# A window-attention kernel: gradient loads on GpSimd's queue, turns by identity matmul, and another order of the products in a pair

## The chip, the cores and the metric

The kernel runs on one core of a Trainium2 chip. The metric is the device time of one execution in microseconds (us); lower is better. "Faster" or "slower" needs 2%; what is nearer counts as "the same".

In the profile PE is TensorE (PEld its weight loads), DVE is VectorE, ACT is ScalarE, POOL is GpSimd and SP is SyncE. SyncE does no arithmetic here: it only issues DMA transfers, one after the other. `SPq`, `POOLq` and `ACTq` are the three engines' issue queues.

## The reference

Attention in windows of 8x8 pixels of a 256x256 image with C = 384 channels, forward and backward, in bf16:

```python
xw  = windows_8x8(x)                       # (1024, 64, 384)
qkv = xw @ wqkv
p   = softmax(einsum('bqc,bkc->bqk', q, k) * C ** -0.5)
o   = einsum('bqk,bkc->bqc', p, v) @ wo    # windows put back into the image
# outputs: o, and the gradients of x, wqkv and wo for a given grad_out
```

## The kernel before

Before the loop the four weight products are folded, so that a window needs only products with 384x384 matrices. The loop takes 4 double windows (128 tokens each, a "quad") per step, 128 steps and a few partial ones at the ends. It is a software pipeline written out by hand: each engine executes its instructions in the order of the program. A step works on three quads at once: `A` is being projected, `B` is in its softmax and its first pair of products, `C_` gets its second pair.

`x` and `grad_out` come in as tiles `xq` and `dq`; DMA transposes turn them into `xT` and `dT`, and the projected `yz` into `tok`. All these are issued by SyncE. Results leave through `osb` and `dsb`, stored by GpSimd. Every PSUM tile comes out of one ring of 8 banks, one bank a tile, so a matmul that starts a tile waits until the bank's last user has been copied out.

```python
    ob = ctx.enter_context(tc.tile_pool(name="ob", bufs=3))      # osb (tag "o") and dsb (tag "d"): 3 each
    ring = ctx.enter_context(tc.tile_pool(name="ring", bufs=8, space=bass.MemoryType.PSUM))
    # ... cut; G_ON_PE is 0, so the loop over grad_turn below does nothing ...
    def load(st):
        bp, t0 = st["at"]
        st["xq"] = xq = grp.tile([P, QUAD, C], BF16, tag="xq", name="xq", bufs=2 * GQ + 4)
        st["dq"] = dq = qp.tile([P, QUAD, C], BF16, tag="dq", name="dq", bufs=6)
        for t in range(QUAD):
            nc.sync.dma_start(out=xq[:, t, :], in_=dram_tile(x, bp, t0 + t))
            nc.sync.dma_start(out=dq[:, t, :], in_=dram_tile(grad_out, bp, t0 + t))

    def load_turn(st):
        xq, dq = st["xq"], st["dq"]
        st["xT"] = xT = qp.tile([P, QUAD, CK, P], BF16, tag="xT", name="xT", bufs=3)
        st["dT"] = dT = qp.tile([P, QUAD, CK, P], BF16, tag="dT", name="dT")
        for src, dst in ((dq, dT), (xq, xT)):
            k = G_ON_PE if src is dq else 0
            if k < QUAD:
                nc.sync.dma_start_transpose(out=dst[:, k:].rearrange("p t m k -> p (t m) k"),
                                            in_=src[:, k:].rearrange("p t c -> p (t c)"))

    # ... cut: project (TensorE, dT or xT -> yz), to_tokens (SyncE, yz -> tok), scores, soft, uv ...

    def turn(st, kind):
        n = ("PT", "ST")[kind]
        st[n] = dst = qp.tile([P, QUAD, WT], BF16, tag=n, name=n)
        pt = ring.tile([P, QUAD, WT], BF16, tag="r")
        for t in range(QUAD):
            for w, o, h in ((0, LO, HI), (1, HI, LO)):
                if kind == 0:
                    nc.tensor.transpose(pt[o, t, :], st["Pb"][o, t, :], ident[o, o])
                else:
                    nc.tensor.transpose(pt[o, t, :], st["ps"][h, w, t, :], ident[h, h])
        nc.vector.tensor_copy(out=dst[:], in_=pt[:])

    def attend(st, pair):
        bp, t0 = st["at"]
        if pair[0] == 0:
            st["Uq"] = grp.tile([P, QUAD, C], BF16, tag="Uq", name="Uq")
            st["Wq"] = grp.tile([P, QUAD, C], BF16, tag="Wq", name="Wq")
        pds = []
        for t in pair:
            pd = ring.tile([P, C], F32, tag="r", name="pd")
            for w, o in ((0, HI), (1, LO)):
                nc.tensor.matmul(pd[o, :], lhsT=st["ps"][:, w, t, :], rhs=st["tok"][:, :, t, w, :], start=True,
                                 stop=False)
            pds.append(pd)

        def both(t, straight, crossed):
            for h, o, (dst, lhs, rhs, first) in ((LO, LO, straight), (LO, HI, crossed), (HI, LO, crossed),
                                                 (HI, HI, straight)):
                nc.tensor.matmul(dst[o, :], lhsT=st[lhs][h, t, :], rhs=st[rhs][h, t, :], start=first, stop=True)

        for t, pd in zip(pair, pds):
            po = ring.tile([P, C], F32, tag="r", name="po")
            pu = ring.tile([P, C], F32, tag="r", name="pu")
            pw = ring.tile([P, C], F32, tag="r", name="pw")
            both(t, (pu, "ST", "xq", True), (po, "PT", "uq", True))
            osb = ob.tile([P, C], BF16, tag="o")
            ENG[EV["o"][t]](out=osb[:], in_=po[:])
            ENG[EV["U"][t]](out=st["Uq"][:, t, :], in_=pu[:])
            both(t, (pw, "Pb", "dq", True), (pd, "ST", "vq", False))
            dsb = ob.tile([P, C], BF16, tag="d")
            ENG[EV["d"][t]](out=dsb[:], in_=pd[:])
            for dst, src in ((out_0, osb), (out_1, dsb)):
                for h, w in ((LO, 1), (HI, 0)):
                    nc.gpsimd.dma_start(out=dram_tile(dst, bp, t0 + t)[WIN * w:WIN * (w + 1)], in_=src[h, :])
            ENG[EV["W"][t]](out=st["Wq"][:, t, :], in_=pw[:])

    # ... cut: gf_group, whose parts ("fillers") are 12 matmuls and one fp32 addition to GF_acc on VectorE ...

    def step(c, b, a):
        # ... cut ...
        C_, B, A = on(c), on(b), on(a)
        B(scores)
        B(soft, 0)
        B(uv, 0, 0)
        B(uv, 0, 1)
        B(soft, 1)
        B(uv, 1, 0)
        B(uv, 1, 1)
        B(soft, 2)
        B(soft, 3)
        B(uv, 2, 0)
        B(uv, 2, 1)
        for t in range(QUAD):
            A(grad_turn, t)
        B(uv, 3, 0)
        B(uv, 3, 1)
        B(soft, 4)
        for mo in range(CK):
            A(project, 0, mo)
        B(soft, 5)
        filler(1)
        C_(attend, (2, 3))
        B(turn, 0)
        B(turn, 1)
        for mo in range(CK):
            A(project, 1, mo)
        A(to_tokens)
        filler(1)
        B(attend, (0, 1))

    # copies out of PSUM: "A" ScalarE, "D" VectorE
    EV = {"z": "AAA", "y": "AAA", "u": "AAAA", "v": "AAAA", "o": "AAAA", "U": "DDDD", "W": "DDDD", "d": "AAAA"}
```

The products in `attend` use the 128x128 array in three ways. The score and projection matmuls use all of it. `po`, `pu`, `pw` and half of `pd` are 64x64 products, four of which run side by side. The other half of `pd` has 128 rows and 64 columns: the "K=128 products".

Of the kernel before, what the change touches and what calls it, by code (L numbers as in the profile page):

```python
# [11 lines left out]
BF16 = mybir.dt.bfloat16  # L12
F32 = mybir.dt.float32

P = 128
WIN = 8
WT = WIN * WIN
QUAD = 4
# [4 lines left out]
def kernel(  # L23
# [21 lines left out]
    nc = tc.nc  # L45
    _, H, W, C = x.shape
# [13 lines left out]
    ring = ctx.enter_context(tc.tile_pool(name="ring", bufs=8, space=bass.MemoryType.PSUM))  # L60

    ident = const.tile([P, P], BF16)
# [8 lines left out]
    for jm in range(JK):  # L71
        pt = ring.tile([P, C], BF16, tag="r")
# [4 lines left out]
    for mo in range(CK):  # L77
        pt = ring.tile([P, C], BF16, tag="r")
# [8 lines left out]
    for dst, left, lo, right, ro, sc in (  # L87
# [5 lines left out]
        for mr in range(CK):  # L93
            pc = ring.tile([P, C], F32, tag="r")
            for mc in range(CK):
                nc.tensor.matmul(pc[:], lhsT=left[:, lo + mc, mr * P:(mr + 1) * P], rhs=right[:, ro + mc, :],
                                 start=(mc == 0), stop=(mc == CK - 1))
# [8 lines left out]
    def dram_tile(ap, bp, t):  # L106
        return ap[0, 2 * WIN * bp:2 * WIN * (bp + 1), WIN * t:WIN * (t + 1), :]

    LO, HI = slice(0, WT), slice(WT, P)
    OTHER = {0: HI, WT: LO}  # L110
# [4 lines that stand above are left out]
        st["dq"] = dq = qp.tile([P, QUAD, C], BF16, tag="dq", name="dq", bufs=6)  # L115
        for t in range(QUAD):
            nc.sync.dma_start(out=xq[:, t, :], in_=dram_tile(x, bp, t0 + t))  # L117
            nc.sync.dma_start(out=dq[:, t, :], in_=dram_tile(grad_out, bp, t0 + t))  # L118

    def load_turn(st):  # L120
        xq, dq = st["xq"], st["dq"]
# [16 lines left out]
    ENG = {"D": nc.vector.tensor_copy, "A": nc.scalar.copy}  # L138
# [31 lines left out]
    def over_k(ap, n=P):  # L170
        return ap.unsqueeze(2).broadcast_to([n, QUAD, WT])

    def soft(st, step):
        sd = st["sd"]
        if step == 0:
# [47 lines left out]
    def turn(st, kind):  # L223
        n = ("PT", "ST")[kind]
        st[n] = dst = qp.tile([P, QUAD, WT], BF16, tag=n, name=n)
        pt = ring.tile([P, QUAD, WT], BF16, tag="r")
        for t in range(QUAD):
            for w, o, h in ((0, LO, HI), (1, HI, LO)):
                if kind == 0:
                    nc.tensor.transpose(pt[o, t, :], st["Pb"][o, t, :], ident[o, o])  # L230
                else:
                    nc.tensor.transpose(pt[o, t, :], st["ps"][h, w, t, :], ident[h, h])
        nc.vector.tensor_copy(out=dst[:], in_=pt[:])

    def attend(st, pair):
        bp, t0 = st["at"]
        if pair[0] == 0:
            st["Uq"] = grp.tile([P, QUAD, C], BF16, tag="Uq", name="Uq")
            st["Wq"] = grp.tile([P, QUAD, C], BF16, tag="Wq", name="Wq")
        pds = []  # L240
        for t in pair:
            pd = ring.tile([P, C], F32, tag="r", name="pd")
            for w, o in ((0, HI), (1, LO)):
                nc.tensor.matmul(pd[o, :], lhsT=st["ps"][:, w, t, :], rhs=st["tok"][:, :, t, w, :], start=True,  # L244
                                 stop=False)
            pds.append(pd)

        def both(t, straight, crossed):
            for h, o, (dst, lhs, rhs, first) in ((LO, LO, straight), (LO, HI, crossed), (HI, LO, crossed),
                                                 (HI, HI, straight)):  # L250
                nc.tensor.matmul(dst[o, :], lhsT=st[lhs][h, t, :], rhs=st[rhs][h, t, :], start=first, stop=True)  # L251

        for t, pd in zip(pair, pds):
            po = ring.tile([P, C], F32, tag="r", name="po")
            pu = ring.tile([P, C], F32, tag="r", name="pu")
            pw = ring.tile([P, C], F32, tag="r", name="pw")
            both(t, (pu, "ST", "xq", True), (po, "PT", "uq", True))
            osb = ob.tile([P, C], BF16, tag="o")
            ENG[EV["o"][t]](out=osb[:], in_=po[:])  # L259
            ENG[EV["U"][t]](out=st["Uq"][:, t, :], in_=pu[:])  # L260
            both(t, (pw, "Pb", "dq", True), (pd, "ST", "vq", False))
            dsb = ob.tile([P, C], BF16, tag="d")
            ENG[EV["d"][t]](out=dsb[:], in_=pd[:])  # L263
            for dst, src in ((out_0, osb), (out_1, dsb)):
                for h, w in ((LO, 1), (HI, 0)):
                    nc.gpsimd.dma_start(out=dram_tile(dst, bp, t0 + t)[WIN * w:WIN * (w + 1)], in_=src[h, :])  # L266
            ENG[EV["W"][t]](out=st["Wq"][:, t, :], in_=pw[:])  # L267

    fill = []

# [12 lines left out]
    def filler(n):  # L283
        while n and fill:
            try:
                next(fill[0])
                n -= 1
            except StopIteration:
                fill.pop(0)

    def step(c, b, a):


        def on(st):
            return (lambda f, *r: f(st, *r)) if st is not None else (lambda f, *r: None)
# [18 lines that stand above are left out]
            A(project, 0, mo)  # L314
        B(soft, 5)
        filler(1)
        C_(attend, (2, 3))
        B(turn, 0)
        B(turn, 1)
        for mo in range(CK):  # L320
            A(project, 1, mo)
        A(to_tokens)
        filler(1)
        B(attend, (0, 1))

    G_ON_PE = 0
    EV = {"z": "AAA", "y": "AAA", "u": "AAAA", "v": "AAAA", "o": "AAAA", "U": "DDDD", "W": "DDDD", "d": "AAAA"}
    quads = [(bp, t0) for bp in range(NBP) for t0 in range(0, NT, QUAD)]
    sts = [{"at": q, "i": i} for i, q in enumerate(quads)]
    n = len(sts)  # L330
    AHEAD = 3
    with tc.manual_schedule(engines=MANUAL):
        for i in range(min(AHEAD, n)):
            load(sts[i])
            if i < AHEAD - 1:
                load_turn(sts[i])
        held = []
        get = lambda i: sts[i] if 0 <= i < n else None
        for i in range(-1, n + 1):
            if AHEAD <= i + AHEAD < n:  # L340
                load(sts[i + AHEAD])
            if AHEAD - 1 <= i + AHEAD - 1 < n:
                load_turn(sts[i + AHEAD - 1])
            step(get(i - 1), get(i), get(i + 1))
            if i > 0:
                held.append(sts[i - 1])
                sts[i - 1] = None
            if held and (len(held) == GQ or i == n):
                fill.append(gf_group(held))
                held = []  # L350
        filler(1 << 30)
# [3 lines left out]
    for f in range(2):  # L355
        nc.vector.tensor_copy(out=GFb[:, f, :, :], in_=GF_acc[:, f, :, :])
        for mb in range(CK):
            pt = ring.tile([P, C], BF16, tag="r")
# [4 lines left out]
    for ma in range(CK):  # L363
        for i, (lhs, f, rhs, r0) in enumerate(((GFT, 0, w_sb, C), (GFb, 0, w_sb, 0), (GFT, 1, woT_sb, 0))):
            pe = ring.tile([P, C], F32, tag="r")
            for mb in range(CK):
                nc.tensor.matmul(pe[:], lhsT=lhs[:, f, mb, ma * P:(ma + 1) * P], rhs=rhs[:, mb, r0:r0 + C],
                                 start=(mb == 0), stop=(mb == CK - 1))
# [6 lines left out]
    for mc in range(CK):  # L375
        pe = ring.tile([P, C], F32, tag="r")
        for ma in range(CK):
            nc.tensor.matmul(pe[:], lhsT=w_sb[:, ma, 2 * C + mc * P:2 * C + (mc + 1) * P], rhs=GFb[:, 1, ma, :],
                             start=(ma == 0), stop=(ma == CK - 1))
# [32 lines left out]
```

## Time and profile before

| before | |
|---|---|
| time, median of 3 runs | 2145.26 us (2143.43 to 2146.45) |
| TensorE busy | 95% of the span |
| from the start of one step's score matmuls to the next | fastest 15.785, median 16.108, mean 16.389 us |
| sum of SyncE's DMA issues | 2006 us |
| TensorE idle before the first matmul that reads dT | 54.2 us |

The steps are those 123 in which every stage has work; they are read off the timeline. First, four lines of the page of the kernel before. The last is from the list of DMA issues: size of one transfer, and median us from issue to landing.

```profile
span 2144.9 us, 50954 instructions
PE 2029.8 (95%) x18814; PEld 1098.6 (51%) x18814; DVE 1379.5 (64%) x3235; ACT 1448.5 (68%) x3213; POOL 1137.8 (53%) x2054
...
L147 PE MATMUL pj<-dT,BT_sb 128*128 128x512 bf16 x1152 | 276.6, 387 | 60.4 <-DMA dT<-dq 54.2
...
dq<-in_grad_out_dram SPq DMA_DIRECT2D x512, 96.0 KB, 3.3
```

TensorE is nearly always busy, and of its idle time one group alone has 60.4 us, 54.2 of them ended by the transpose that makes dT. The view of waits (who waits, for whom: total us, times, longest) shows that beside another, much larger wait:

```profile
PE pj L147 <- DMA dT<-dq: 54.2, 58, 3.4
...
ACT osb L259 <- DMA out_dram<-osb: 180.6, 84, 2.4
...
ACT dsb L263 <- DMA out_dram<-dsb: 6.4, 6, 2.6
```

By this label ScalarE spends 180.6 us waiting for an `osb` buffer whose store has not landed. The label is an inference of the view (it names whatever event came last), and here it is wrong: followed one by one in the trace, the last store from the same buffer had landed at least 3.5 us before each of these 84 copies, and the copy began a median 0.09 us after the last matmul into its `po` had ended. ScalarE, busy for 68%, was waiting for TensorE. For `dsb` the 6 waits are real waits for a buffer by this test: each copy began within 0.2 us of the landing of the store from its own buffer.

Why is dT late? Here is SyncE's queue over one step, in the timeline (start us, duration us, engine, line, operation, count, and in brackets idle time before it, of which there is none here):

```profile
1006.75 6.27 SPq L156 DMA_TRANSPOSE tok<-yz  x1
1013.06 0.59 SPq L117 DMA_DIRECT2D xq<-in_x_dram  x1
1013.69 0.60 SPq L118 DMA_DIRECT2D dq<-in_grad_out_dram  x1
...
1018.20 2.17 SPq L127 DMA_TRANSPOSE dT<-dq  x1
1020.42 1.99 SPq L127 DMA_TRANSPOSE xT<-xq  x1
1022.51 5.35 SPq L156 DMA_TRANSPOSE tok<-yz  x1
```

Each issue starts 0.04 to 0.10 us after the one before it has ended: the queue has no pause at all. Summed over the run: tok 703, xT 362, xq 335, dq 323, dT 282, with three single transfers 2006 us of 2145. SyncE is a second engine at its limit, beside TensorE, though the page counts it as no engine at all.

Last, the end of a pair and the next step's scores, in the timeline:

```profile
1001.44 0.35 PE L251 MATMUL po<-uq,PT 64*64 64x384 bf16 x2
...
1001.88 0.48 ACT L259 CAST osb<-po 128x384 bf16<-128x384 f32 x1 [2.15 <-DMA out_dram<-osb]
...
1001.96 0.33 PE L251 MATMUL pd<-vq,ST 64*64 64x384 bf16 x2
...
1002.41 0.28 PE L165 MATMUL sd<-xT,yz 128*128 128x64 bf16 x4
```

The last products start at 1001.96, the scores only 0.45 us later. They begin 0.05 us after ScalarE has finished `osb` (1001.88 + 0.48 = 1002.36): by this a wait for a PSUM bank, though it looks like the price of a change of array mode. The copy itself began 0.09 us after `po` was finished (1001.44 + 0.35 = 1001.79); the store that its label names was not that of its buffer, which had landed at 996.07.

### The profile page before, as it was taken

To read this page: it belongs to the slowest core of one execution; us is meant where nothing else is said; L and a number is where in the kernel's file an instruction comes from. 1 tells how busy PE (TensorE), PEld (TensorE's weight loads), DVE (VectorE), ACT (ScalarE), POOL (GpSimd) and SP (SyncE) were. 2 spreads that over 40 slices of the span, in tenths; PEclk is the share of its full clock that TensorE was granted. 3 is DMA by queue.
4 is the path that set the end of the run, shared out by engine and by line. 5 is a ranking of instruction groups with operands and counts; after the bars stand their busy time and mean duration, and the time that the engine had idled before them with its cause. 6 is when DMAs were issued, how large, how long until landed. Compare 5 with 4: busy or idle time off the path is not lost.

```text
span 2144.9 us, 50954 instructions
## 1 busy us (share of the span) xinstructions
PE 2029.8 (95%) x18814; PEld 1098.6 (51%) x18814; DVE 1379.5 (64%) x3235; ACT 1448.5 (68%) x3213; POOL 1137.8 (53%) x2054
## 2 busy tenths in 40 slices
PE   7899999999999999999999999999999999999998
PEld 4455555555555555555545555554555555455544
DVE  4566666666666666666666666666666666666665
ACT  5676676767666766666766767676766667676663
POOL 1555555555555555555554555555555455555544
PEclk9999999999999999999999999999999999999999
DMA  8999999999999999999999999999999999999992
GB/s 171 198 192 197 192 196 196 192 193 199 193 193 196 200 191 195 191 196 193 198 190 190 198 191 202 193 197 188 197 198 196 190 198 194 192 198 194 190 184 76
DMA packets 1046330, 409.04 MB, mean 191 GB/s; under 512 B 880704, under 2 KB 1028928, under 8 KB 1046080
## 3 DMA queue, kind: packets, MB, share of 16 engines
q1 hardware_dynamic: 947376, 304.17, 80.9%
q0 software_dynamic: 98304, 101.32, 18.2%
q8 instruction: 147, 2.41, 0.5%
q14 instruction: 103, 0.84, 0.1%
q10 hardware_dynamic: 400, 0.29, 0.0%
HBM read 101.84 MB, written 101.84 MB: 95 GB/s over the span
## 4 chain that ended last, share of the span: by engine, by line
PE 41%; DMA 26%; SPq 15%; ACT 9%; issue 5%; POOL 1%; DVE 1%; ACTq 0%; POOLq 0%
DMA dT<-dq 20%; PE pj L147 16%; PE pj L219 10%; PE pg L278 9%; SPq L117 7%; SPq L118 7%; DMA out_dram<-osb 5%; ACT yz L150 4%; ACT osb L259 3%; PE sd L165 3%; POOL out_dram L266 1%; SPq L156 1%; DMA out_dram<-dsb 1%; ACT yz L152 1%; PE pd L244 1%
## 5 line engine op out<-in xcount | busy, mean ns | idle before, releaser
L266 POOL DMA_DIRECT2D out_dram<-osb x1024 | 571.9, 563 | 933.6 <-ACT osb L259 906.3
L266 POOL DMA_DIRECT2D out_dram<-dsb x1024 | 571.9, 563 | 51.2 <-issue 20.5
L259 ACT CAST osb<-po 128x384 bf16<-128x384 f32 x512 | 249.8, 488 | 408.4 <-DMA out_dram<-osb 180.6
L280 DVE TENSOR_TENSOR GF_acc<-pg,GF_acc 128x384 f32<-128x384 f32 x258 | 143.9, 558 | 542.7 <-PE pg L278 542.7
L278 PEld LDWEIGHTS <-xq 128*128 128x128 bf16 x3072 | 300.0, 98 | 226.8 <-issue 1.6
L219 PEld LDWEIGHTS <-xT 128*128 128x128 bf16 x3072 | 291.9, 98 | 185.5 <-issue 3.6
L219 PE MATMUL pj<-B_sb,xT 128*128 128x384 bf16 x1536 | 334.6, 327 | 1.8 <-ACT dsb L263 1.8
L219 PE MATMUL pj<-AT_sb,xT 128*128 128x384 bf16 x1536 | 334.0, 327 | 0.0
L147 PE MATMUL pj<-dT,BT_sb 128*128 128x512 bf16 x1152 | 276.6, 387 | 60.4 <-DMA dT<-dq 54.2
L260 DVE CAST Uq<-pu 128x384 bf16<-128x384 f32 x512 | 283.0, 553 | 75.3 <-PE pu L251 75.3
L267 DVE CAST Wq<-pw 128x384 bf16<-128x384 f32 x512 | 280.5, 548 | 0.0
L221 ACT CAST uq<-pj 128x384 bf16<-128x384 f32 x512 | 247.5, 483 | 41.9 <-PE pj L219 37.5
L278 PE MATMUL pg<-Uq,xq 128*128 128x384 bf16 x1536 | 270.5, 326 | 0.1
L278 PE MATMUL pg<-Wq,xq 128*128 128x384 bf16 x1536 | 270.1, 326 | 0.1
L147 PE MATMUL pj<-xT,A_sb 128*128 128x512 bf16 x1152 | 269.2, 379 | 0.6
L263 ACT CAST dsb<-pd 128x384 bf16<-128x384 f32 x512 | 254.7, 497 | 7.6 <-DMA out_dram<-dsb 6.4
L221 ACT CAST vq<-pj 128x384 bf16<-128x384 f32 x512 | 250.2, 489 | 2.8 <-PE pj L219 0.5
L152 ACT CAST yz<-pj 128x512 bf16<-128x512 f32 x384 | 224.2, 585 | 32.0 <-PE pj L147 0.9
L150 ACT CAST yz<-pj 128x512 bf16<-128x512 f32 x384 | 208.4, 638 | 14.4 <-PE pj L147 13.3
L147 PEld LDWEIGHTS <-BT_sb 128*128 128x128 bf16 x1152 | 106.8, 99 | 207.2 <-DMA dT<-dq 92.2
L198 ACT COPY ps<-Pb 64x256 bf16<-64x256 bf16 x256 | 103.2, 403 | 149.6 <-DVE Pb L195 148.1
L251 PE MATMUL pu<-xq,ST 64*64 64x384 bf16 x1024 | 175.5, 336 | 0.0
(64 smaller groups left out, 2217.4 us busy)
## 6 DMA issues: line engine op xcount, KB each, us to landing
xq<-in_x_dram SPq DMA_DIRECT2D x512, 96.0 KB, 3.2
dq<-in_grad_out_dram SPq DMA_DIRECT2D x512, 96.0 KB, 3.3
out_dram<-osb POOLq DMA_DIRECT2D x1024, 48.0 KB, 3.8
out_dram<-dsb POOLq DMA_DIRECT2D x1024, 48.0 KB, 4.4
dT<-dq SPq DMA_TRANSPOSE x128, 6.5
xT<-xq SPq DMA_TRANSPOSE x128, 7.1
tok<-yz SPq DMA_TRANSPOSE x128, 7.9
w_sb<-in_wqkv_dram SPq DMA_DIRECT2D x1, 864.0 KB, 5.5
```

Of the source, the lines that this page charges most:

```text
L147: nc.tensor.matmul(pj[:].rearrange("p t w k -> p (t w k)"), lhsT=wgt[:, m, mo * P:(mo + 1) * P], rhs=src[:, :, m, :], start=(m == 0), stop ...
L150: ENG[EV["z"][mo]](out=yz[:, mo, :, 0:4:3, :], in_=pj[:])
L152: ENG[EV["y"][mo]](out=yz[:, mo, :, 1:3, :], in_=pj[:])
L219: nc.tensor.matmul(pj[:], lhsT=st["xT"][:, t, m, :], rhs=wgt[:, m, :], start=(m == 0), stop=(m == CK - 1))
L221: cp(out=dst[:, t, :], in_=pj[:])
L251: nc.tensor.matmul(dst[o, :], lhsT=st[lhs][h, t, :], rhs=st[rhs][h, t, :], start=first, stop=True)
L259: ENG[EV["o"][t]](out=osb[:], in_=po[:])
L260: ENG[EV["U"][t]](out=st["Uq"][:, t, :], in_=pu[:])
L263: ENG[EV["d"][t]](out=dsb[:], in_=pd[:])
L266: nc.gpsimd.dma_start(out=dram_tile(dst, bp, t0 + t)[WIN * w:WIN * (w + 1)], in_=src[h, :])
L267: ENG[EV["W"][t]](out=st["Wq"][:, t, :], in_=pw[:])
L278: nc.tensor.matmul(pw[:], lhsT=st["xq"][:, t, ma * P:(ma + 1) * P], rhs=st["UW"[f] + "q"][:, t, :], start=(i == 0), stop=(i == n - 1))
```

## The change

The intent has two parts. The gradient loads leave SyncE's full queue for GpSimd's. And in a pair of tiles the products are put in an order that is meant to have fewer changes of array mode: the turns of P and dS, now identity matmuls, come first, then all 64x64 products, then the K=128 products, so that the output `dsb` (the gradient of x) is finished, copied and stored last.

```diff
--- before.py
+++ after.py
@@ -115,7 +115,7 @@
         st["dq"] = dq = qp.tile([P, QUAD, C], BF16, tag="dq", name="dq", bufs=6)
         for t in range(QUAD):
             nc.sync.dma_start(out=xq[:, t, :], in_=dram_tile(x, bp, t0 + t))
-            nc.sync.dma_start(out=dq[:, t, :], in_=dram_tile(grad_out, bp, t0 + t))
+            nc.gpsimd.dma_start(out=dq[:, t, :], in_=dram_tile(grad_out, bp, t0 + t))
 
     def load_turn(st):
         xq, dq = st["xq"], st["dq"]
@@ -223,48 +223,45 @@
     def turn(st, kind):
         n = ("PT", "ST")[kind]
         st[n] = dst = qp.tile([P, QUAD, WT], BF16, tag=n, name=n)
-        pt = ring.tile([P, QUAD, WT], BF16, tag="r")
+        pt = ring.tile([P, QUAD, WT], F32, tag="r", name="pt")
         for t in range(QUAD):
             for w, o, h in ((0, LO, HI), (1, HI, LO)):
-                if kind == 0:
-                    nc.tensor.transpose(pt[o, t, :], st["Pb"][o, t, :], ident[o, o])
-                else:
-                    nc.tensor.transpose(pt[o, t, :], st["ps"][h, w, t, :], ident[h, h])
+                lhs, h = (st["Pb"][o, t, :], o) if kind == 0 else (st["ps"][h, w, t, :], h)
+                nc.tensor.matmul(pt[o, t, :], lhsT=lhs, rhs=ident[h, h], start=True, stop=True)
         nc.vector.tensor_copy(out=dst[:], in_=pt[:])
+
+    def store(dst, src, bp, t):
+        for h, w in ((LO, 1), (HI, 0)):
+            nc.gpsimd.dma_start(out=dram_tile(dst, bp, t)[WIN * w:WIN * (w + 1)], in_=src[h, :])
 
     def attend(st, pair):
         bp, t0 = st["at"]
         if pair[0] == 0:
             st["Uq"] = grp.tile([P, QUAD, C], BF16, tag="Uq", name="Uq")
             st["Wq"] = grp.tile([P, QUAD, C], BF16, tag="Wq", name="Wq")
-        pds = []
+        def both(straight, crossed):
+            for h, o, (dst, lhs, rhs, done) in ((LO, LO, straight), (LO, HI, crossed), (HI, LO, crossed),
+                                                (HI, HI, straight)):
+                nc.tensor.matmul(dst[o, :], lhsT=st[lhs][h, t, :], rhs=st[rhs][h, t, :], start=True, stop=done)
+
+        made = []
         for t in pair:
-            pd = ring.tile([P, C], F32, tag="r", name="pd")
-            for w, o in ((0, HI), (1, LO)):
-                nc.tensor.matmul(pd[o, :], lhsT=st["ps"][:, w, t, :], rhs=st["tok"][:, :, t, w, :], start=True,
-                                 stop=False)
-            pds.append(pd)
-
-        def both(t, straight, crossed):
-            for h, o, (dst, lhs, rhs, first) in ((LO, LO, straight), (LO, HI, crossed), (HI, LO, crossed),
-                                                 (HI, HI, straight)):
-                nc.tensor.matmul(dst[o, :], lhsT=st[lhs][h, t, :], rhs=st[rhs][h, t, :], start=first, stop=True)
-
-        for t, pd in zip(pair, pds):
-            po = ring.tile([P, C], F32, tag="r", name="po")
-            pu = ring.tile([P, C], F32, tag="r", name="pu")
-            pw = ring.tile([P, C], F32, tag="r", name="pw")
-            both(t, (pu, "ST", "xq", True), (po, "PT", "uq", True))
+            po, pu, pw, pd = [ring.tile([P, C], F32, tag="r", name=n) for n in ("po", "pu", "pw", "pd")]
+            both((pu, "ST", "xq", True), (po, "PT", "uq", True))
             osb = ob.tile([P, C], BF16, tag="o")
             ENG[EV["o"][t]](out=osb[:], in_=po[:])
             ENG[EV["U"][t]](out=st["Uq"][:, t, :], in_=pu[:])
-            both(t, (pw, "Pb", "dq", True), (pd, "ST", "vq", False))
+            both((pw, "Pb", "dq", True), (pd, "ST", "vq", False))
+            ENG[EV["W"][t]](out=st["Wq"][:, t, :], in_=pw[:])
+            made.append((t, pd))
+            store(out_0, osb, bp, t0 + t)
+        for t, pd in made:
+            for w, o in ((0, HI), (1, LO)):
+                nc.tensor.matmul(pd[o, :], lhsT=st["ps"][:, w, t, :], rhs=st["tok"][:, :, t, w, :], start=False,
+                                 stop=True)
             dsb = ob.tile([P, C], BF16, tag="d")
             ENG[EV["d"][t]](out=dsb[:], in_=pd[:])
-            for dst, src in ((out_0, osb), (out_1, dsb)):
-                for h, w in ((LO, 1), (HI, 0)):
-                    nc.gpsimd.dma_start(out=dram_tile(dst, bp, t0 + t)[WIN * w:WIN * (w + 1)], in_=src[h, :])
-            ENG[EV["W"][t]](out=st["Wq"][:, t, :], in_=pw[:])
+            store(out_1, dsb, bp, t0 + t)
 
     fill = []
 
@@ -314,9 +311,9 @@
             A(project, 0, mo)
         B(soft, 5)
         filler(1)
-        C_(attend, (2, 3))
         B(turn, 0)
         B(turn, 1)
+        C_(attend, (2, 3))
         for mo in range(CK):
             A(project, 1, mo)
         A(to_tokens)
```

## The prediction

> **What bounds it now.** Part 1 of the page has TensorE busy for 95%, but the 128 near-equal steps tell more. From one step's score matmuls to the next (timeline), the fastest quarter take 15.79 us, the mean is 16.39. Nearly all of the 0.60 us between, 76 us in the run, is idle before one matmul, the first that reads dT (waits view: PE for DMA dT<-dq 54 us, 58 times). The transposes come late because the SyncE queue is full: its issues, added up over the timeline, take 703 (tok) + 362 (xT) + 335 (xq) + 323 (dq) + 282 (dT) = 2006 us, with some 0.04 us between them 16.2 us a step. So SyncE sets the pace and TensorE, at 15.79, is just under it.
>
> **Loads moved.** This takes 4 x 0.63 = 2.5 us a step off SyncE, leaving 13.6 us, below TensorE. The Trainium skill ("DMA: Bandwidth & Descriptors", Issuing engines are not separate DMA queues) says another issuer saves only issue time; here that is the limit. dT, xT and tok should be issued several us earlier and the dT wait should go: up to -76 us, perhaps -68 with what stays at the start. GpSimd has 16 stores of 0.56 us a step, 9 us; a load has twice the rows, so I estimate 1 us each, 13 us in all, with a pause of about 6 us in its stores where they fit.
>
> **Order changed.** The tempting reading is that fewer changes of array mode save PE time. The skill ("TensorEngine Tiling (Array Packing)", Key Properties) says a change of mode drains the array; the trace agrees: entering a 64-wide mode costs 0.09 us beyond streaming, leaving the identity turn for 128x128 about 0.16. But two long gaps (0.45 us from the last 64x64 product to the turn, and to the scores) are waits for a PSUM bank, the matmul starting 0.05 us after ScalarE finishes osb. The new order moves them.
> - Pair (2,3): in the built program the last pw takes the bank of the P turn, the last pd that of the first po. The P copy (fp32, estimated 0.42 us for 0.28) queues behind the 0.56 us GF_acc addition, and osb ends 0.97 us after the first product starts. So the fourth product group waits till 1.45 us after the last filler matmul starts, not 1.1. Then 0.26 + 0.19 (K=128) and 0.32 into the projection: 2.2 us against 2.06 now.
> - Pair (0,1): the last pd waits for GF_acc (0.96); scores start at 1.74 against 1.67.
> Together +0.1 to +0.3 us a step, +13 to +38 us. The larger VectorE copies are off the path.
>
> **Sum.** 2145 - 68 + 26 = 2103 us; 8 in 10 between 2078 and 2130. Faster by over 2% (below 2102) 0.47, within 2% 0.50, slower 0.03.
>
> **What would show it.** dT waits under 15 us; SyncE idle before tok; the fastest steps at about 16.0 us, the mean within 0.1 of that; new PE waits in the fourth product group, for VectorE's PT copy or ScalarE's osb; GpSimd 65-70% busy, about 1 us a load; before the scores about 0.32 us, not 0.45.
>
> **What would make it wrong.** If transposes are slowed by the DMA engines rather than by issue, dT waits stay: about 2150. If a gradient load takes 2 us on GpSimd, stores come late and osb buffers block ScalarE. If turn and products, now in one mode, overlap better, or K=128 to 128x128 is cheap, steps get under 15.8: near 2070.

## The result

The changed kernel took 2119.73 us, the median of 4 runs (2112.48 to 2125.33), against 2144.35 for the kernel before (4 runs, 2136.02 to 2146.45). The ratio is 0.9895, with a 95% interval of 0.9865 to 0.9926: about 1% faster, which counts as the same. Here and below a ratio is formed from fast runs alone; it is not quite the ratio of the medians quoted.

The page of the kernel after, the same parts as before, with three groups that are new or changed:

```profile
span 2110.7 us, 50826 instructions
...
PE 2065.2 (98%) x18814; PEld 1093.3 (52%) x18814; DVE 1391.3 (66%) x3235; ACT 1474.2 (70%) x3213; POOL 1422.0 (67%) x2566
...
L118 POOL DMA_DIRECT2D dq<-in_grad_out_dram x512 | 273.2, 542 | 69.0 <-PE pj L147 34.9
...
L147 PE MATMUL pj<-dT,BT_sb 128*128 128x512 bf16 x1152 | 271.4, 381 | 0.7 <-DMA dT<-dq 0.7
...
dq<-in_grad_out_dram POOLq DMA_DIRECT2D x512, 96.0 KB, 5.3
```

The wait for dT fell from 54.2 to 0.7 us. One gradient load occupies GpSimd for 0.54 us (0.63 on average on SyncE before), but lands 5.3 us after its issue, not 3.3. The waits:

```profile
PE pj L147 <- DMA dT<-dq: 0.7, 1, 0.7
...
POOL out_dram L235 <- DMA out_dram<-osb: 67.8, 100, 2.2
...
ACT osb L252 <- DMA out_dram<-osb: 22.3, 23, 2.7
...
ACT dsb L263 <- DMA out_dram<-dsb: 50.7, 33, 5.5
...
PE pj L219 <- ACT dsb L263: 15.7, 13, 3.2
```

These waits of ScalarE are for buffers, all 56 by the test above: for `osb` they grew from none to 22.3 us, for `dsb` from 6.4 to 50.7, and TensorE now waits behind `dsb`, at a projection that needs a PSUM bank which ScalarE has not yet emptied into `dsb`. SyncE has room: its issues sum to 1533 us, and it is idle before `tok` 124 times, for 471 us in all. The issue of a `tok` started a median 6.30 us after the last copy into its `yz` in the kernel before, and 0.03 us after it now: the transposes no longer stand in line.

The steps say what came of it. The fastest is 15.850 us (before 15.785), the median 15.854, but the mean is 16.143: most steps are at the limit, and 21 of the 123 are longer by 0.1 to 6.2 us. Here is one of those, first GpSimd's queue and then the engines that wait:

```profile
1315.79 1.72 POOL L235 DMA_DIRECT2D out_dram<-osb  x3 [0.76 <-ACT osb L252]
1318.44 0.56 POOL L235 DMA_DIRECT2D out_dram<-osb  x1 [0.92 <-DMA out_dram<-dsb]
1319.21 1.12 POOL L235 DMA_DIRECT2D out_dram<-dsb  x2 [0.21 <-ACT yz L152]
1321.83 1.12 POOL L235 DMA_DIRECT2D out_dram<-dsb  x2 [1.50 <-DMA dq<-in_grad_out_dram]
1322.95 2.23 POOL L235 DMA_DIRECT2D out_dram<-osb  x4
```

```profile
1323.05 0.48 ACT L263 CAST dsb<-pd 128x384 bf16<-128x384 f32 x1
...
1325.78 0.48 ACT L263 CAST dsb<-pd 128x384 bf16<-128x384 f32 x1 [2.24 <-DMA out_dram<-dsb]
...
1326.31 0.48 PE L219 MATMUL pj<-AT_sb,xT 128*128 128x384 bf16 x2 [0.99 <-ACT dsb L263]
```

Four `osb` stores are issued before the first `dsb` store of the pair, and the queue pauses for earlier transfers to land, once for a gradient load. (GpSimd's transfers take eight completion semaphores in turn, and nearly all of these pauses end 0.28 or 0.55 us after the previous transfer on the same semaphore has landed. The loads make it 20 transfers a step instead of 16.) By the order of the program the stores issued at 1319.21 are of the buffer that the second copy shown needs, three tiles on; ScalarE gets it at 1325.78 after 2.24 us, and TensorE stands for 0.99 us. Of the seven `dsb` stores in this stretch, the slowest landed 5.9 us after issue.

In an undisturbed step the pair (2,3) looks like this (timeline):

```profile
1153.19 0.56 DVE L277 TENSOR_TENSOR GF_acc<-pg,GF_acc 128x384 f32<-128x384 f32 x1 [1.09 <-PE pg L275]
...
1153.63 1.08 ACT L252 CAST osb<-po 128x384 bf16<-128x384 f32 x2 [0.27 <-PE po L245]
1153.67 0.41 DVE L231 CAST PT<-pt 128x256 bf16<-128x256 f32 x1
...
1153.80 0.35 PE L245 MATMUL po<-uq,PT 64*64 64x384 bf16 x2
...
1154.13 0.32 PE L245 MATMUL pw<-dq,Pb 64*64 64x384 bf16 x1
...
1154.16 0.35 PE L245 MATMUL pd<-vq,ST 64*64 64x384 bf16 x2
...
1154.45 0.52 PE L260 MATMUL pd<-tok,ps 128*64 128x384 bf16 x4
```

The second `po` starts 0.05 us after VectorE's GF_acc addition ends (1153.19 + 0.56 = 1153.75), the last `pw` 0.05 us after the copy of `PT` does (1153.67 + 0.41 = 1154.08), and the last `pd` 0.05 us after the first `osb` copy does (1153.63 + 0.48 = 1154.11). The long wait between the last products and the turn is gone, and these have come in its place. Taken as the median over the fast steps, from the start of the last filler matmul to the projection it is 2.058 us before and 2.067 after; in the pair (0,1), to the scores, 1.676 and 1.707. The remaining 0.025 us of the longer step lie in the two stretches between, 0.013 each.

### The profile page after: what moved, and what is told of

It is laid out like the page before. It is cut to its first block, busy times and chain, and to the rows that moved or that the text cites. A ratio compares the mean times of both kernels' runs of the same rounds, so it can differ in the third digit from the quotient of the medians.

```text
span 2110.7 us, 50826 instructions
## 1 busy us (share of the span) xinstructions
PE 2065.2 (98%) x18814; PEld 1093.3 (52%) x18814; DVE 1391.3 (66%) x3235; ACT 1474.2 (70%) x3213; POOL 1422.0 (67%) x2566
## 4 chain that ended last, share of the span: by engine, by line
PE 79%; DMA 8%; ACT 6%; issue 3%; POOL 2%; DVE 1%; ACTq 0%; POOLq 0%; SPq 0%
PE pj L147 20%; PE pg L275 20%; PE pj L219 19%; PE pd L260 5%; DMA out_dram<-dsb 4%; PE sd L165 4%; PE pu L245 4%; PE pw L245 4%; DMA dq<-in_grad_out_dram 2%; POOL out_dram L235 2%; PE pd L245 2%; ACT vq L221 2%; ACT yz L150 1%; PE po L245 1%; ACT uq L221 1%
## 5 line engine op out<-in xcount | busy, mean ns | idle before, releaser
L235 POOL DMA_DIRECT2D out_dram<-osb x1024 | 577.8, 571 | 487.9 <-ACT osb L252 429.1
L252 ACT CAST osb<-po 128x384 bf16<-128x384 f32 x512 | 238.5, 484 | 282.9 <-PE pu L245 206.5
L118 POOL DMA_DIRECT2D dq<-in_grad_out_dram x512 | 273.2, 542 | 69.0 <-PE pj L147 34.9
L263 ACT CAST dsb<-pd 128x384 bf16<-128x384 f32 x512 | 226.7, 481 | 90.9 <-DMA out_dram<-dsb 50.7
L147 PE MATMUL pj<-dT,BT_sb 128*128 128x512 bf16 x1152 | 271.4, 381 | 0.7 <-DMA dT<-dq 0.7
L245 PE MATMUL pw<-dq,Pb 64*64 64x384 bf16 x1024 | 212.9, 329 | 0.0
```

The lines of the kernel that those rows point to most:

```text
L118: nc.gpsimd.dma_start(out=dq[:, t, :], in_=dram_tile(grad_out, bp, t0 + t))
L147: nc.tensor.matmul(pj[:].rearrange("p t w k -> p (t w k)"), lhsT=wgt[:, m, mo * P:(mo + 1) * P], rhs=src[:, :, m, :], start=(m == 0), stop ...
L235: nc.gpsimd.dma_start(out=dram_tile(dst, bp, t)[WIN * w:WIN * (w + 1)], in_=src[h, :])
```

## The experiments

My theory after the result: the loads gain what was predicted, and most of it is given back because `dsb` is now copied and stored last, while three buffers are too few for stores that come late. Rivals: the order's own cost in each step is the larger part; or the loads gain less on GpSimd than predicted, through slower landing; or the dT wait was a matter of DMA bandwidth and not of issue time. Ten kernels were run, all correct. The first four ran beside each other on one chip, as did e5 to e8, and e9 with e10; each has its ratio to the kernel before in its own rounds, three of them (one for e8). The table has them all; the waits (us) are TensorE's for dT, and ScalarE's for `osb` and `dsb` buffers by the test above. What the view puts down to `osb` stores beyond these (180.6 us in the kernel before, 30.6 of 47.6 in e1, 3.3 of 4.9 in e2, 30.1 in e4, 6.8 in e9, 34.4 in e10, and more in e3 and e6 to e8) was no wait for a buffer.

| kernel | median us | ratio to before (95%) | fastest / mean step us | dT | osb | dsb |
|---|---|---|---|---|---|---|
| before | 2145.26 | 1 | 15.785 / 16.389 | 54.2 | 0 | 6.4 |
| after | 2119.73 | 0.9895 (0.9865–0.9926) | 15.850 / 16.143 | 0.7 | 22.3 | 50.7 |
| e1 loads only | 2081.80 | 0.9740 (0.9717–0.9764) | 15.785 / 15.931 | 0.4 | 17.0 | 18.3 |
| e2 order only | 2138.31 | 1.0015 (0.9988–1.0042) | 15.852 / 16.309 | 28.6 | 1.6 | 39.1 |
| e3 after, 4 buffers | 2077.84 | 0.9725 (0.9705–0.9746) | 15.897 / 15.916 | 1.9 | 0 | 0 |
| e4 loads only, 4 buffers | 2066.06 | 0.9668 (0.9646–0.9690) | 15.785 / 15.793 | 0.5 | 0 | 1.9 |
| e5 after, 4 dsb buffers | 2090.65 | 0.9764 (0.9748–0.9781) | 15.895 / 15.954 | 1.4 | 30.2 | 0 |
| e6 e3 with transposes | 2075.06 | 0.9691 (0.9676–0.9705) | 15.886 / 15.895 | 2.4 | 0 | 0 |
| e7 loads on ScalarE | 2726.91 | 1.2731 (1.2710–1.2752) | 15.786 / 21.110 | 0 | 0 | 19.6 |
| e8 SyncE loaded more | 2373.12 | 1.1082 (1.1060–1.1104) | 15.789 / 18.134 | 210.6 | 0 | 1.2 |
| e9 before, 4 buffers | 2142.04 | 1.0017 (0.9978–1.0056) | 15.785 / 16.292 | 48.2 | 0 | 0 |
| e10 e4, one osb copy split | 2092.89 | 0.9772 (0.9747–0.9797) | 16.017 / 16.026 | 0.2 | 0 | 0 |

### e1: the loads alone

```diff
-            nc.sync.dma_start(out=dq[:, t, :], in_=dram_tile(grad_out, bp, t0 + t))      # in before
+            nc.gpsimd.dma_start(out=dq[:, t, :], in_=dram_tile(grad_out, bp, t0 + t))
```

> The kernel before with only the gradient loads moved to GpSimd. Theory 1 (SyncE's full queue was the pace; what is left over in the changed kernel is ScalarE waiting for one of the 3 output buffers because GpSimd now has the loads between the stores): dT waits under 10 us, fastest steps 15.79 us as before, waits of osb or dsb for a store of 20 to 60 us as in the changed kernel, time 2085 to 2110 us. Rival 2 (the left-over waits come from the new order, which stores dsb later): no such waits, about 2070 to 2078 us. Rival 3 (the new order gives part of the gain through fewer array modes): clearly slower than the changed kernel, over 2130 us.

It took 2081.80 us, 2.6% less than before, and so is faster than the whole change. The dT wait is gone and the fastest step is what it was, 15.785 us. But the mean is 0.146 us above it, and ScalarE waits 17.0 us for `osb` buffers and 18.3 for `dsb`: even in the old order, three buffers are short once GpSimd carries the loads.

### e2: the order alone

```diff
-            nc.gpsimd.dma_start(out=dq[:, t, :], in_=dram_tile(grad_out, bp, t0 + t))    # in after
+            nc.sync.dma_start(out=dq[:, t, :], in_=dram_tile(grad_out, bp, t0 + t))
```

> The kernel changed in order alone, gradient loads left on SyncE. Theory 1: SyncE still sets the pace, so the mean step stays at about 16.4 us, dT waits of 40 to 90 us stay, time 2140 to 2152 us, no gain; fastest steps 15.85 us. Rival 3 (order gives part of the gain): 2115 to 2130 us.

2138.31 us, a ratio of 1.0015: nothing. That does not make the order free. Its fastest step is 15.852 us against 15.785, and the waits for `dsb` are already there at 39.1 us, with no load on GpSimd; but SyncE still sets the pace and dT is still waited for (28.6 us). A delay that falls inside that wait shows in no time; that it did so here is argued, not shown.

### e3: the whole change with four output buffers

```diff
-    ob = ctx.enter_context(tc.tile_pool(name="ob", bufs=3))      # in after
+    ob = ctx.enter_context(tc.tile_pool(name="ob", bufs=4))
```

> The changed kernel with 4 instead of 3 buffers for each of osb and dsb (4 is one step's worth, so a buffer comes back a whole step later). Theory 1: waits of osb and dsb for a store fall from 73 us to under 10 us, the mean step falls from 16.11 to within 0.05 us of the fastest 15.85, time 2076 to 2085 us. If instead GpSimd itself is what is late (it waits for a landing before it reuses a semaphore), the extra buffers only soften it: 2090 to 2105 us. If the left-over is DMA bandwidth, no change: 2112 to 2125 us.

2077.84 us. One number was changed, and the wait for `dsb` is gone:

```profile
ACT dsb L263 <- DMA out_dram<-dsb: 1.3, 6, 0.2
```

The mean step is now 0.019 us above the fastest. (The view also puts 71.5 us before `osb` copies down to `dsb` stores; no copy there began near the landing of its own buffer's store, and TensorE waits for none of them.) GpSimd still waits some 135 us for earlier transfers to land, against 120 in the changed kernel and 27 in the kernel before; with a fourth buffer that lateness costs next to nothing. So the buffers are the cause of the long steps, and the late stores matter only through them.

### e4: the loads alone with four output buffers

```diff
-    ob = ctx.enter_context(tc.tile_pool(name="ob", bufs=3))      # in e1
+    ob = ctx.enter_context(tc.tile_pool(name="ob", bufs=4))
```

> Old order, gradient loads on GpSimd, 4 output buffers each. Theory 1: nothing but TensorE's own 15.79 us a step is left, 2068 to 2078 us, about 8 us (127 steps x 0.07 us) faster than the new order with 4 buffers. Rival 3: slower than the new order with 4 buffers by 10 us or more.

2066.06 us, 3.3% less than before: the best version found, in the old order. Its page and waits:

```profile
span 2061.3 us, 51453 instructions
...
PE 2009.0 (97%) x18814; PEld 1104.9 (54%) x18814; DVE 1380.2 (67%) x3235; ACT 1445.7 (70%) x3213; POOL 1418.7 (69%) x2566
```

```profile
PE pj L147 <- DMA dT<-dq: 0.5, 1, 0.5
...
ACT dsb L263 <- DMA out_dram<-dsb: 1.9, 2, 1.3
```

The mean step is 15.793 us, the fastest 15.785. Note that TensorE is busy for 97% here and for 98% in the slower changed kernel: the same 18814 matmuls are put at 2009.0 us here and 2065.2 there, so the share of busy time does not rank the two. Nor does the 30.1 us that the view still puts down to `osb` stores: those had landed 8.6 us or more before the copies from the same buffers began, and nearly all steps are at the limit.

### e5: four buffers for dsb only

```diff
-            dsb = ob.tile([P, C], BF16, tag="d")      # in after
+            dsb = ob.tile([P, C], BF16, tag="d", bufs=4)
```

> The changed kernel with a fourth buffer for dsb alone, osb left at 3. Theory: the waits that the changed kernel has left over come from dsb alone, because the new order stores the two dsb of a pair last, and with GpSimd also loading, the dsb of three tiles back has not landed. Expected: as with 4 of both, 2075 to 2085 us, stalls at the uv projections gone. If osb's buffers mattered as well: 2090 to 2110 us.

2090.65 us, more than the 2075 to 2085 that I expected, so `osb` mattered too. What is left is in this line:

```profile
ACT osb L252 <- DMA out_dram<-osb: 30.2, 26, 2.9
```

All 26 are waits for a buffer, and TensorE waits 4.8 us behind them, at the projections. By the ratios, the buffers of `dsb` are worth 0.9895 - 0.9764 = 1.3% and those of `osb` another 0.9764 - 0.9725 = 0.4% (28 and 8 us of 2145).

### e6: transposes in place of identity matmuls

```diff
-        pt = ring.tile([P, QUAD, WT], F32, tag="r", name="pt")      # in e3
+        pt = ring.tile([P, QUAD, WT], BF16, tag="r", name="pt")
-                nc.tensor.matmul(pt[o, t, :], lhsT=lhs, rhs=ident[h, h], start=True, stop=True)
+                nc.tensor.transpose(pt[o, t, :], lhs, ident[h, h])
```

> The changed order with 4 buffers of each, P and dS turned by transposes into a bf16 bank (as before) instead of identity matmuls. Theory 1 (what sets the length of pair (2,3) is osb's PSUM bank, and a transpose of 64x64 is no other array mode): the same step as with identity matmuls, 15.90 us within 0.06, time 2072 to 2086 us. Rival (a transpose is a mode of its own and drains the array): 0.1 to 0.3 us more a step, 2090 to 2116 us.

2075.06 us, next to 2077.84 for e3; the fastest steps are 15.886 and 15.897 us. From the start of the first turn to the start of the first product it is 0.147 us in both, with 16 turns between. So a 64x64 transpose followed by a 64x64 product pays no change of mode either, and turning P and dS by matmul brings nothing by itself.

### e7: the loads on ScalarE's queue

```diff
-            nc.sync.dma_start(out=dq[:, t, :], in_=dram_tile(grad_out, bp, t0 + t))      # in before
+            nc.scalar.dma_start(out=dq[:, t, :], in_=dram_tile(grad_out, bp, t0 + t))
```

> The kernel before with the gradient loads on ScalarE's queue instead of GpSimd's. Theory 1 (it is the issue time on SyncE that counts, wherever it goes): dT waits vanish as they do with GpSimd, fastest steps still near 15.79 us; output stores are then undisturbed on GpSimd, so osb and dsb wait for stores under 20 us; but ScalarE, busy 68%, has to issue 4 loads a step, which may hold its PSUM copies up: 2070 to 2110 us. Rival (the gain comes from the other kind of queue on GpSimd): dT waits stay and 2130 to 2150 us.

The expectation failed by far: 2726.91 us, 27% slower. The timeline shows why:

```profile
1007.93 1.67 ACTq L118 DMA_DIRECT2D dq<-in_grad_out_dram  x2
...
1009.64 0.48 ACT L221 CAST uq<-pj 128x384 bf16<-128x384 f32 x1 [6.56 <-DMA xq<-in_x_dram]
...
1010.17 0.48 PE L219 MATMUL pj<-AT_sb,xT 128*128 128x384 bf16 x1 [3.92 <-ACT uq L221]
```

ScalarE did no copy for 6.56 us before 1009.64, because the loads ahead of it in its queue were not free to issue. In the built program each of these loads first waits on one of eight completion semaphores that it shares, in rotation, with SyncE's transfers; so it waits for a transfer of SyncE's: the two loads shown each start 0.02 us after one has landed, the first after a transpose into `tok`, the second after a load of `xq`. TensorE waits for ScalarE's copies, 412.1 us in all. (The granted clock was 0.913 over the run, but the fastest step is 15.786 us, as before.) The kernel measures what a wait in the queue of an engine with work on the path costs; it does not measure ScalarE's issue time, for which it was made.

### e8: more load on SyncE

```diff
             nc.sync.dma_start(out=dq[:, t, :], in_=dram_tile(grad_out, bp, t0 + t))      # in before
+            nc.sync.dma_start(out=sm.tile([P, 32], BF16, tag="junk", name="junk", bufs=8)[:],
+                              in_=dram_tile(x, bp, t0 + t)[:, :, 0:32])
```

> The kernel before with 4 more small loads a step on SyncE, of 8 KB each with the same 128 rows (64 B a row), into a scratch tile that nothing reads. Theory 1 (SyncE's issue time is the pace of the kernel before): each costs about 0.6 us of it, 4 x 0.63 = 2.5 us a step, so the mean step rises to 18.6 to 19.0 us and the time to 2420 to 2480 us. Rival (bytes or the DMA engines are the pace; the added bytes are 4.2 MB of 409): under 2190 us.

The extra transfers are small (8 KB) and nobody reads them. The kernel took 2373.12 us (two runs, 2372.00 and 2374.24), 11% longer, and TensorE's wait for dT rose from 54.2 to 210.6 us. Transfers with a twelfth of a load's bytes lengthened the mean step by 1.75 us, so the issue queue and not the bytes was what bound the kernel before. Nor was it the 16 DMA engines, whose packets the page puts at 99.7% of the span in the kernel before: in e8 it is 88.4% while the kernel is slower, and in e4 the same bytes come to 104.9% while it is faster. The size was off: four issues at 0.67 us would be 2.7 us, and 2.5 was expected. SyncE's issues sum to 2212 us here, 207 more than before, though the new ones alone take 342; the transposes' issues had become shorter by about 0.9 us a step. In the changed kernel too: `tok` took 4.34 us to issue on average, 5.50 before. What an issue of a transpose waits for inside its own time is open.

### e9: the kernel before with four output buffers

```diff
-    ob = ctx.enter_context(tc.tile_pool(name="ob", bufs=3))      # in before
+    ob = ctx.enter_context(tc.tile_pool(name="ob", bufs=4))
```

> Control: the kernel before with 4 output buffers each and nothing else. Theory 1: SyncE still sets the pace, so the buffers change nothing: 2130 to 2150 us, dT waits of 40 to 90 us, mean step about 16.4 us. If buffers alone were worth the 12 to 16 us that they brought with the old order and loads on GpSimd: 2120 to 2130 us.

2142.04 us, a ratio of 1.0017: the same. The 180.6 us of the view have all but gone, and nothing came of it:

```profile
ACT osb L259 <- DMA out_dram<-osb: 6.8, 5, 2.1
...
PE pj L147 <- DMA dT<-dq: 48.2, 47, 5.0
```

The 180.6 us were ScalarE's own spare time, as the landings said: not one of these waits was for a buffer, with three buffers or with four. This is also the control for e3 and e4: the fourth buffer is worth nothing by itself, and pays only once GpSimd has the loads.

### e10: one osb copy split over two engines

```diff
-            ENG[EV["o"][t]](out=osb[:], in_=po[:])      # in e4, for t == 0
+            nc.scalar.copy(out=osb[:, :C // 2], in_=po[:, :C // 2])
+            nc.vector.tensor_copy(out=osb[:, C // 2:], in_=po[:, C // 2:])
```

> The fastest version so far (old order, loads on GpSimd, 4 buffers) with the first osb copy of pair (0,1) cut in two halves, one on ScalarE and one on VectorE. Claim tested: the 0.45 us in front of the score matmuls is a wait for the PSUM bank that osb's copy frees, not a drain of the array. A half copy should take about 0.35 us in place of 0.48, so the gap shrinks by 0.10 to 0.15 us and the fastest step goes from 15.79 to 15.63 to 15.70 us, time 2048 to 2058 us, unless VectorE, 0.35 us later with the other copies, holds up the softmax. Rival (a drain): the gap stays 0.45 us and the time 2063 to 2070 us.

It was to shorten the copy that the scores wait for. It took 2092.89 us, slower than e4, and the fastest step went up from 15.785 to 16.017:

```profile
1004.91 0.32 ACT L260 CAST osb<-po 128x192 bf16<-128x192 f32 x1 [2.15 <-PE pu L251]
1005.26 0.36 DVE L261 CAST osb<-po 128x192 bf16<-128x192 f32 x1 [0.58 <-ACT osb L260]
...
1005.67 0.86 PE L165 MATMUL sd<-xT,yz 128*128 128x64 bf16 x24 [0.36 <-DVE osb L261]
```

The two halves did not run together: VectorE began 0.03 us after ScalarE had ended, released by it. The copy took longer in all, and the scores again began 0.05 us after the last reader of the bank had finished. The direction was the opposite of the expected one, but it answers the question: the gap before the scores grew from 0.45 to 0.69 us with nothing changed in the array's modes, so it is a wait for the bank.

## Why the prediction was right and wrong

The time, predicted as 2103 us between 2078 and 2130, was 2119.73; the likeliest single class, within 2%, is the one that came, though with 0.50 against 0.47 for "faster" that says little. The sum was near only because a cost was left out and another was put too high. The ratios show it:

| ratio to before | 3 buffers | 4 buffers |
|---|---|---|
| loads on SyncE, old order | 1 | 1.0017 |
| loads on GpSimd, old order | 0.9740 | 0.9668 |
| loads on SyncE, new order | 1.0015 | not run |
| loads on GpSimd, new order | 0.9895 | 0.9725 |

In us of 2145: with buffers enough, the loads bring 3.3%, 71 us, and the order takes 0.57%, 12 us (0.9725 - 0.9668). The third buffer's shortage takes 0.72%, 15 us, in the old order (0.9740 - 0.9668), and 1.7%, 36 us, in the new one (0.9895 - 0.9725). Then -71 + 12 + 36 = -23 us, which is 1.05% of 2145; the three add up by the way they are formed, so the sum is an account and no check. The prediction had -68 and +26 and nothing for buffers: two misses of opposite sign, so that its time came near by luck. (The changed kernel's ratio is from other runs of the kernel before than the rest, with an interval of about 6 us to either side; its own runs differ by 13 us, and why they spread more than those of the other kernels is open.)

- **SyncE is the limit and dT its sign: right.** e8 and e1 show it from both sides. "dT waits under 15 us" came as 0.7, and the pauses before `tok` are there. (The "nearly all" of 76 us that it laid to dT is 54 in the view.) The Trainium skill ("DMA: Bandwidth & Descriptors", section "Issuing engines are not separate DMA queues") says that issuing on several engines saves only the time of issue, which is "usually small relative to the DMA itself". The trace agrees with the first half: a load lands no sooner on GpSimd (5.3 us after issue, 3.3 on SyncE). The second holds for one plain load (0.63 us of issue, 3.3 to the landing), less so for a transpose (`tok`: 5.50 of 7.9), and it says nothing of a queue: the issues summed to 2006 of 2145 us.
- **"perhaps -68" for the loads: right only with a fourth buffer** (71 us); with three, e1 gained 2.6%, 55 us.
- **The step that failed is "with a pause of about 6 us in its stores where they fit", and with it "the mean within 0.1 of that".** No term of the sum stood for output buffers. The danger was named for the other case, a load of 2 us ("stores come late and osb buffers block ScalarE"), and left out of the sum, which put the issue time at 1 us. It measured 0.54, better than predicted, GpSimd was busy for 67% as predicted, and still the stores came late: they wait for earlier transfers to land (120 us in all, 27 before), and `dsb`, last in the new order, is stored behind four `osb` stores. The mean was 0.29 us above the fastest step, which over 128 steps is 37 us. e3 and e5 show that buffers cure it.
- **The order's cost, "+0.1 to +0.3 us a step", entered as 26 us: too large as a length of the step, too small as an effect.** With three buffers the order took 33 us in all (0.9895 - 0.9740), most of it through the buffers. The fastest step grew by 0.065 us with three buffers, 8 us in all, and by 0.11 with four. The mechanism held: the last products do wait for the banks of GF_acc, `PT` and `osb`, of which `osb` and the `pd` behind it also moved together in e3, where `osb` started 0.044 us later and the last `pd` 0.045 later. The terms that were mis-sized, for pair (2,3): the fourth group, predicted to wait "till 1.45 us after the last filler matmul starts", started after 1.34, and "0.32 into the projection" was 0.259. So the pair took 2.067 us, not 2.2. Before the scores it was 0.258, not 0.32, and pair (0,1) took 1.707, not 1.74.
- **"Fewer changes of array mode save PE time" was rightly distrusted.** The Trainium skill ("TensorEngine Tiling (Array Packing)", Key Properties) says that changing the mode drains the array. A change does cost something here: the first 64x64 turn starts 0.256 us after the last filler matmul, where the next matmul of the same kind would start after 0.163. But what stood in the gap before the scores was a bank wait (e10), as by the same 0.05 us after `osb` in the gap before the turn, which no run tested, and the new order put other bank waits in their place. Nor are the changes fewer, counted in the timeline: in either order a pair goes from the whole array to two other shapes and back, three changes, since a turn by transpose is no change (e6).

## What to carry to other kernels

Add up the issue times on each DMA queue before trusting a TensorE that is 95% busy: here a full queue without a line of its own on the page set the pace, and moving a sixth of it away gained 3.3%. The engine that takes the transfers over delays its other users, so give their buffers one more copy in the same edit (one number here, worth 36 us in the changed kernel), and be wary of an order that copies and stores one output last (the third buffer's shortage took 36 us in it, 15 in the old order). A wait's label is an inference: before acting on it, look whether the very buffer's transfer landed just before. None of 180.6 us put down to stores of `osb` was a wait for a buffer; the 50.7 us of `dsb` were, and curing them gained 28 us.

## What the Trainium skill lacked or had wrong

- "DMA: Bandwidth & Descriptors", "Issuing engines are not separate DMA queues": issue time is called usually small relative to the DMA itself. For one plain load it was (0.63 us, 3.3 to the landing), for `tok` not (5.50 of 7.9), and added up on SyncE it was 2006 us of 2145; four more small transfers a step made the kernel 11% slower. No page that I read gives the issue time of a DMA transpose; `tok` occupied the queue for 5.50 us on average before and 4.34 after, `dT` for 2.20 and 2.02.
- The same page calls SyncE's and ScalarE's path generally faster than GpSimd's. For a 96 KB load that holds for landing (3.3 us after issue on SyncE before, 5.3 on GpSimd after, where a load of the same size on SyncE took 4.1), not for the time the issuing engine is held (0.63 and 0.54 us).
- No page that I read spells out for a kernel's author that a transfer issued on ScalarE holds up the copies behind it, and may wait for another engine's transfers through completion semaphores used in rotation: e7, 27% slower, with ScalarE kept from copying for 6.56 us in the example.
- "TensorEngine Tiling (Array Packing)", Key Properties, gives no size for the drain. Here it was 0.09 us beyond streaming into 64x64, 0.258 us from the start of the last K=128 product to a matmul over the whole array, and nothing seen between 64x64 transposes and 64x64 products (0.147 us from the first turn to the first product in both forms, e6).
- "PSUM — Partial Sum Buffer", "PSUM bank collisions raise a hardware error", says to guard PSUM by the bank (times quadrant) with semaphores, two readers included; e10 agrees in that VectorE's half was released by ScalarE's. It gives no number for what the guard costs: 0.05 us from the last copy's end to the matmul, and for the two halves 0.32 and 0.36 us one after the other with 0.03 between, where one whole copy takes 0.48.
